# DeltaNet and a two-level mixture of experts: scaled values on VectorE, query masks on GpSimd, scores one chunk further ahead

## The chip, the cores and the metric

The kernel runs on one core of one Trainium2 chip. The metric is device time in microseconds (us) of one execution of the whole program. Four names of engines recur: TensorE (PE in the profile; its weight loads are PEld), VectorE (DVE), ScalarE (ACT) and GpSimd (POOL). SyncE (SP) only issues transfers.

## The reference

Attention first: for each of 4 batches and 8 heads, a 48 by 48 state is carried over 768 steps. Then each of the 3072 rows of 384 numbers goes to one of 16 experts, chosen in two steps (group, then expert in the group). The code is condensed.

```python
k_n = k / (np.linalg.norm(k, axis=-1, keepdims=True) + 1e-06)
for t in range(S):                                     # 768 steps
    y[:, :, t] = q[:, :, t] @ state                    # per batch and head
    v_old = k_n[:, :, t] @ state
    state = state + beta[:, :, t] * outer(k_n[:, :, t], v[:, :, t] - v_old)
x = y.transpose(0, 2, 1, 3).reshape(3072, 384)
g_idx = argmax(x @ w_group)                            # softmax weight g_w
e_idx = argmax(x @ w_expert[g_idx])                    # softmax weight e_w
out[i] = g_w * e_w * (relu(x[i] @ w1[g, e]) @ w2[g, e])
```

## The kernel before

The 768 steps are cut into 24 chunks (`NCH`) of 32 steps (`C`). All 4 batches of a chunk lie on the 128 partitions, 32 each; the 8 heads lie along the free axis, two to a pair. Inside a chunk the recurrence is turned into matrix products, with one triangular 32 by 32 inverse per batch and head. The inverses of four chunks (`RG`) are made together by a generator, `inverse(g)`, as a long row of small VectorE operations; GpSimd makes the square roots of the key norms for it (the result is `nrm`, turned over into `normt`).

One chunk `u` has these steps, in the names of the profile:

- `g_ps` (L278, `gram`): scores of the keys and queries of chunk `u + LEAD` against its keys, made some chunks ahead. They use one buffer, `kqd`, filled by two transfers of 256 KB. ScalarE copies them out as `gt` (keys, for the inverse) and `gq` (queries), both at L288.
- `gqm` (L298, L303, `mask`): the query scores with the upper triangle cut away. For early chunks each is spread to twice the width, with zeros in the half that belongs to the other batch of a pair, so that one product serves two batches.
- `a_ps` (L460, `begin_a`): the values times the negated key norm, eight ScalarE instructions, one for a head, each 128 by 48, written into PSUM. Then (L472) TensorE adds the products of keys and old state to them. ScalarE copies the sum out as `f` (L478).
- `o_ps` (L483): queries times old state.
- `w_ps` (L491): the inverse `mt` times `f`; copied out as `w` (L494).
- `s_ps` (L501): the state products, keys times `w`; copied out as `s_bd` (L507, two instructions). The next chunk's `a_ps` and `o_ps` products read `s_bd`.
- `o_ps` again (L514, or L519 for late chunks): masked query scores times `w`; copied out as `x` (L523), which is the attention output.
- `t_ps`, `xt`, `l_ps`, `lg` (L541 to L554, `logits`): the routing logits of chunk `u - 1`. Every four chunks a ranking product (`hots` and `acc`, into the bank of `l_ps`) is added, and `route(r)` picks the experts by small operations on VectorE and GpSimd. `s_ps` at L703 are small products that sort rows by expert.

The order on each engine's queue is written out by hand: the loop `for u in range(NCH + 1)` (L870) calls the pieces in order, and each engine runs its own instructions strictly in that order. `work(n)` puts as many steps of the running `inverse` and `route` generators into the queues as a budget allows; `allow(...)` releases a generator that holds at a named point. The chunk loop has two forms: one for chunks whose scores are still being made ahead (`if ahead_of[u]`), and an `else` form, in which the logits of the chunk before stand ahead of `w_ps` and of the state products.

PSUM has eight banks. The state `s_ps` takes four; before, `g_ps`, `o_ps`, `t_ps`/`l_ps` have one each, and one (tag `s`) is shared by `a_ps` and `w_ps`.

After the loop the rows are sorted by expert and 16 experts are run one after another (`h_ps`, L1076, and `y_ps`, L1095), fed by transfers of 3 MB of weights for each.

## Time and profile before

| | |
|---|---|
| device time, median of 3 runs | 556.77 us (556.64 to 562.29) |
| the profiled execution: own time, span | 556.0 us, 554.2 us |
| busy: PE, PEld, DVE, ACT, POOL | 477.0, 448.5, 228.1, 211.0, 188.3 us |
| mean granted TensorE clock | 0.926 |
| chunk 1's first state read to the first expert product | 46.9 to 282.9 us |

How to read it: busy time of PE counts modelled ends of pipelined matmuls. A number in brackets after an instruction is the idle time of its engine ahead of it and what ended that. "issue" is time in which an engine waited for nothing that the profile shows. PEclk is the clock that TensorE was granted as a part of the full one. An instruction shown as 32 by 96 "x32" is 32 matmul records; the program lists them as 16, since each fp32 product takes two passes.

### The profile page before, as it was taken

What the parts mean: (1) busy time and instruction counts of PE and PEld (TensorE: products, weight loads), DVE (VectorE), ACT (ScalarE), POOL (GpSimd) and SP (SyncE); (2) the same over time, 40 slices, a digit from 0 to 9 for tenths busy, and PEclk for the clock granted to TensorE, in tenths of its full rate; (3) what the DMA queues carried; (4) which work ended last, traced back from release to release, by engine and by line L of the source; (5) the groups of instructions that cost most, each with busy time, mean ns of one, the idle gap of its engine ahead of it and who ended that gap; (6) DMA issues with size and microseconds to landing.
All of it is one profiled execution on the core that took longest, in us unless ns stands there. A gap on an engine that the chain in (4) does not pass through costs nothing.

```text
span 554.2 us, 19014 instructions
## 1 busy us (share of the span) xinstructions
PE 477.0 (86%) x8124; PEld 448.5 (81%) x8124; DVE 228.1 (41%) x850; ACT 211.0 (38%) x541; POOL 188.3 (34%) x326
## 2 busy tenths in 40 slices
PE   3456888887788776877999999999999999999993
PEld 3346777777777775766799999999999999999993
DVE  3999669189387495412381011101121110111110
ACT  3336675586667566665421111111111111111110
POOL 3040021161341440400114464445653545545322
PEclk9998887799788787787799999999999999999998
DMA  5666665666547343410129878776986788988741
GB/s 168 225 210 165 167 203 149 160 200 171 198 135 227 100 135 95 141 53 17 56 68 311 275 248 286 229 236 217 318 275 209 257 262 282 312 296 258 235 170 34
DMA packets 59593, 107.35 MB, mean 194 GB/s; under 512 B 19438, under 2 KB 41897, under 8 KB 59507
## 3 DMA queue, kind: packets, MB, share of 16 engines
q1 hardware_dynamic: 53587, 96.11, 55.1%
q0 software_dynamic: 5920, 10.00, 5.8%
q8 instruction: 65, 1.06, 0.8%
q14 instruction: 21, 0.17, 0.1%
HBM read 91.97 MB, written 14.27 MB: 192 GB/s over the span
## 4 chain that ended last, share of the span: by engine, by line
PE 50%; DMA 18%; ACT 15%; issue 9%; SPq 4%; DVE 1%; POOL 1%; DVEq 0%; POOLq 0%; ACTq 0%
PE y_ps L1095 11%; PE h_ps L1076 11%; ACT a_ps L460 8%; DMA y_dram<-yq 5%; DMA out_dram<-yo,to_i 5%; PE a_ps L472 5%; PE g_ps L278 4%; PE o_ps L483 4%; DMA yr<-y_dram 4%; PE w_ps L491 4%; SPq L1135 4%; PE l_ps L446 3%; ACT s_bd L507 3%; DMA kqt<-in_kq_dram 2%; PE s_ps L256 2%
## 5 line engine op out<-in xcount | busy, mean ns | idle before, releaser
L1095 PE MATMUL y_ps<-hid,w 128*128 128x224 f32 (+15 forms) x768 | 132.9, 332 | 0.7 <-issue 0.3
L1095 PEld LDWEIGHTS y_ps<-hid,w 128*128 128x128 f32 x768 | 128.9, 190 | 1.8 <-ACT yt L1100 0.8
L1076 PE MATMUL h_ps<-xt,w 128*128 128x232 f32 (+14 forms) x720 | 122.7, 330 | 0.0
L1076 PEld LDWEIGHTS h_ps<-xt,w 128*128 128x128 f32 x720 | 120.1, 190 | 0.3
L1048 POOL DMA_INDIRECT xq<-x_dram,from_q x92 | 87.6, 952 | 34.2 <-issue 25.0
L1079 ACT ACTIVATE hid<-h_ps 128x448 f32<-128x448 f32 (+15 forms) x64 | 32.1, 501 | 99.3 <-PE h_ps L1076 81.2
L1107 POOL DMA_INDIRECT out_dram<-yo,to_i x32 | 34.1, 1064 | 94.4 <-DVE yo L1145 82.4
L1098 DVE COPY yt<-y_ps 128x232 f32<-128x232 f32 (+13 forms) x14 | 5.1, 366 | 140.2 <-PE y_ps L1095 127.7
L460 ACT ACTIVATE a_ps<-kv,normt 128x48 f32<-128x48 f32 x184 | 56.0, 304 | 6.0
L1100 ACT ACTIVATE yt<-y_ps 128x224 f32<-128x224 f32 (+15 forms) x34 | 11.4, 336 | 118.9 <-PE y_ps L1095 91.2
L472 PE MATMUL a_ps<-s_bd,kqt 128*32 128x96 f32 x736 | 29.9, 318 | 12.9 <-ACT s_bd L507 11.2
L507 ACT ACTIVATE s_bd<-s_ps 48x768 f32<-48x768 f32 x46 | 36.8, 799 | 6.1 <-PE s_ps L501 5.8
L472 PEld LDWEIGHTS a_ps<-s_bd,kqt 128*32 128x32 f32 x736 | 25.3, 148 | 14.7 <-ACT s_bd L507 12.5
L501 PE MATMUL s_ps<-w,kv 32*112 32x96 f32 x736 | 27.0, 285 | 7.6 <-ACT found L846 2.7
L501 PEld LDWEIGHTS s_ps<-w,kv 32*112 32x112 f32 x736 | 22.7, 188 | 11.0 <-ACT w L494 3.3
L256 PE MATMUL s_ps<-kqt 48*32 48x32 f32 (+1 forms) x832 | 14.3, 269 | 20.1 <-issue 7.2
L256 PEld LDWEIGHTS s_ps<-kqt 48*32 48x32 f32 x832 | 11.2, 145 | 22.9 <-issue 8.1
L1145 DVE TENSOR_SCALAR yo<-yr,gate 128x384 f32<-128x384 f32 (+14 forms) x28 | 11.1, 420 | 44.9 <-DMA yr<-y_dram 37.8
L446 PE MATMUL l_ps<-wr,xt 128*128 128x20 f32 x132 | 19.2, 273 | 11.0 <-ACT xt L547 9.8
L483 PE MATMUL o_ps<-s_bd,kqt 128*32 128x96 f32 x736 | 27.8, 306 | 0.0
L446 PEld LDWEIGHTS l_ps<-wr,xt 128*128 128x128 f32 x132 | 16.9, 195 | 13.0 <-ACT xt L547 11.2
L278 PE MATMUL g_ps<-kqd,kqt 128*32 128x128 f32 x480 | 24.3, 356 | 3.0 <-issue 2.1
(174 smaller groups left out, 655.3 us busy)
## 6 DMA issues: line engine op xcount, KB each, us to landing
w<-in_w_dram SPq DMA_DIRECT2D x29, 1536.0 KB
kv<-in_kv_dram SPq DMA_DIRECT2D x24, 448.0 KB
kqt<-in_kq_dram SPq DMA_DIRECT2D x20, 512.0 KB
kqd<-in_kq_dram SPq DMA_DIRECT2D x30, 256.0 KB
x_dram<-x SPq DMA_DIRECT2D x24, 192.0 KB
w<-in_w_dram SPq DMA_DIRECT2D x24, 128.0 KB
y_dram<-yq SPq DMA_DIRECT2D x36, 84.0 KB
yr<-y_dram SPq DMA_DIRECT2D x14, 192.0 KB
```

What stands on the lines that cost most here:

```text
L256: nc.tensor.matmul(g_out[quads[b], hh, j, of], lhsT=kqt[rows, 0, j, quads[b]], rhs=kqt[rows, of, j, quads[b]], start=True, stop=True, skip ...
L278: nc.tensor.matmul(g_ps[quads[b], j], lhsT=kqt[:, 0, j, quads[b]], rhs=kqd_[u % 2][:, :, :, j, quads[b]], start=True, stop=True, skip_grou ...
L446: nc.tensor.matmul(out_, lhsT=lhsT, rhs=rhs, start=first, stop=final, skip_group_check=True)
L460: nc.scalar.activation(a_ps[:, h], v[:, h], ACT.Copy, scale=norm[g][:, uu * H + h:uu * H + h + 1])
L472: nc.tensor.matmul(a_ps[quads[b], 2 * j:2 * j + 2, :], lhsT=kqt[:, 0, j, quads[b]], rhs=s_bd[:, b, j], start=False, stop=True, skip_group_ ...
L483: nc.tensor.matmul(o_ps[quads[b], 2 * j:2 * j + 2, :], lhsT=kqt[:, 1, j, quads[b]], rhs=s_bd[:, b, j], start=(j == 0), stop=False, skip_gr ...
L501: nc.tensor.matmul(s_at[0:KR, b, j], lhsT=k[quads[b], j, 0:KR], rhs=w[quads[b], 2 * j:2 * j + 2], start=(u == 0 and j == 0), stop=True, sk ...
L507: nc.scalar.activation(s_bd[rows, :, :, hh, :], s_at[rows, :, :, hh * D:(hh + 1) * D], ACT.Copy)
L1048: nc.gpsimd.indirect_dma_start(out=xq[:, g, :], out_offset=None, in_=x_dram[:, :].rearrange("n (q c) -> (n q) c", q=4), in_offset=bass.Ind ...
L1076: nc.tensor.matmul(h_ps[:, k], lhsT=w1[:, j, (f + k) * 128:(f + k + 1) * 128], rhs=xt[:, j, 0:R], start=(j == 0), stop=(j == DC - 1), skip ...
L1095: nc.tensor.matmul(y_ps, lhsT=w2[:, f, j * 128:(j + 1) * 128], rhs=hid[:, f], start=(f == 0), stop=(f == FC - 1))
L1107: put = nc.gpsimd.indirect_dma_start(out=out[:, :], out_offset=bass.IndirectOffsetOnAxis(ap=to[0:P, i:i + 1], axis=0), in_=yo[0:P, :], in_ ...
```

## The change

Three pieces of work change engine or place, and one constant moves.

- **Scaled values.** `begin_a(u + 1)` is one VectorE multiplication (128 by 384, the norm spread by a stride of zero) where it was eight ScalarE instructions. It writes into a PSUM bank of its own (tag `a`) and stands at the head of chunk `u`, as soon as `f` of chunk `u` has left that bank. Chunk 0 keeps the eight instructions. Before the loop, three products against the identity write that bank (`a_home`), where before they wrote bank 0 of the state.
- **Query masks.** `mask(u)` is a GpSimd multiplication in place on `gq` (128 by 256), queued at the head of the chunk after the one that made the scores. `spread(u + 1)`, at the head of chunk `u`, is two ScalarE copies (128 by 256 each) with a scale of 0 or 1 for each partition; late chunks need none.
- **Scores.** `LEAD` is 10 where it was 9, with one more `kqt` buffer. `gram(u + LEAD)` stands between the state products and the query products; its bank is the one of `w_ps` (tag `s`), the bank `g` is gone, and its copies stand right behind those of the state.
- **The rest.** The first form of the loop now holds for `u < NCH - 3`, so chunks 14 to 20 move from the `else` form into it. The generators start at other chunks, and GpSimd clears the upper triangles of `m` behind the roots where it did so ahead of them.

```diff
-LEAD = 9
+LEAD = 10
@@ gram, keep_scores
-            g_ps = ps.tile([128, NP, 2, 2, C], F32, tag="g", name=f"g_ps{u}")
+            g_ps = ps.tile([128, NP, 2, 2, C], F32, tag="s", name=f"g_ps{u}")
...
                 g_ps = made.pop(u)
+                unmasked.append(u)
@@ mask
         def mask(u):
-            like = [128, H, 2, C]
-            gqm = wk.tile(like, F32, tag="gqm", name=f"gqm{u}", bufs=3)
+            nc.gpsimd.tensor_tensor(raws[u], raws[u],
+                                    cut["causal"][:, None, :].to_broadcast([128, H, C]),
+                                    op=ALU.mult)
+
+        def spread(u):
             if u >= LATE:
...
-                nc.vector.tensor_tensor(gqs[u], raws.pop(u),
-                                        cut["causal"][:, None, :].to_broadcast([128, H, C]),
-                                        op=ALU.mult)
+                gqs[u] = raws.pop(u)
                 return
-            gqs[u] = gqm
-            nc.vector.tensor_tensor(
-                gqs[u], raws.pop(u)[:, :, None, :].to_broadcast(like),
-                cut["upper"].rearrange("p (a t) -> p a t", a=2)[:, None].to_broadcast(like),
-                op=ALU.mult)
+            gqs[u] = wk.tile([128, H, 2, C], F32, tag="gqm", name=f"gqm{u}")
+            for a in range(2):
+                nc.scalar.activation(gqs[u][:, :, a], raws[u], ACT.Copy,
+                                     scale=cut["parity"][:, a:a + 1])
+            raws.pop(u)
@@ begin_a
+            v = kv_[u % NV][:, H * 64:].rearrange("p (h d) -> p h d", h=H)
+            by = norm[g][:, uu * H:(uu + 1) * H]
             if u:
-                a_ps = ps.tile([128, H, D], F32, tag="s", name=f"a_ps{u}")
+                a_ps = ps.tile([128, H, D], F32, tag="a", name=f"a_ps{u}")
+                nc.vector.tensor_tensor(a_ps, v, by[:, :, None].to_broadcast([128, H, D]),
+                                        op=ALU.mult)
             else:
                 a_ps = wk.tile([128, H, D], F32, tag="f", name="f0")
-            for h in range(H):
-                nc.scalar.activation(a_ps[:, h], v[:, h], ACT.Copy,
-                                     scale=norm[g][:, uu * H + h:uu * H + h + 1])
+                for h in range(H):
+                    nc.scalar.activation(a_ps[:, h], v[:, h], ACT.Copy, scale=by[:, h:h + 1])
@@ before the loop
+            for u in range(2 * RG):
+                mask(u)
...
             for u in range(2 * RG, LEAD):
                 early_gram(u, homes[u % len(homes)])
                 begin(after_gram[u])
+                mask(u)
+            spread(0)
@@ the loop over chunks
-                if 0 < u < NCH - 1:
-                    mask(u + 1)
                 if u:
                     next(step)
...
-                keep_scores()
-                if u % RG == RG - 1 and u // RG + 2 < NGR:
-                    start(inverse(u // RG + 2), SHARE)
+                if u + 1 < NCH:
+                    begin_a(u + 1)
+                    spread(u + 1)
+                for v in unmasked:
+                    mask(v)
+                unmasked.clear()
...
-                if ahead_of[u]:
+                if u < NCH - 3:
                     work(10)
                     next(step)
-                    begin_a(u + 1)
                     next(turned)
...
                     next(step)
+                    for v in ahead_of[u]:
+                        gram(v)
+                    keep_scores()
+                    if u % RG == 1 and u // RG + 2 < NGR:
+                        start(inverse(u // RG + 2), SHARE)
                     work(9)
+                    allow(ROOTS)
                     next(step)
                     next(turned)
                     allow(PE_STEP)
                     allow(ACT_STEP)
-                    for v in ahead_of[u]:
-                        gram(v)
                 else:
...
                     next(step)
-                    if u + 1 < NCH:
-                        begin_a(u + 1)
```

ScalarE's queue in chunk 2 before, from the copy `f` of chunk 2 (line, operation, output<-inputs, shape):

```order
L478 ACTIVATE f_1221<-a_ps_1080 128x384
L288 ACTIVATE gt_749<-g_ps_1147 128x2x4x32
L288 ACTIVATE gq_1241<-g_ps_1147 128x2x4x32
L494 ACTIVATE w_1286<-w_ps_1253 128x384
L460 ACTIVATE a_ps_1288<-kv_117,normt_594 128x48 x8
L547 ACTIVATE xt_1301<-t_ps_1297 128x384
L507 ACTIVATE s_bd<-s_ps 48x16x48 x2
L523 ACTIVATE x_1345<-o_ps_1223 128x384
L554 ACTIVATE lg_1089<-l_ps_1347 128x20
```

The same chunk on ScalarE now:

```order
L488 ACTIVATE f_1245<-a_ps_1067 128x384
L305 ACTIVATE gqm_1266<-gq_571,con 128x8x32 x2
L504 ACTIVATE w_1336<-w_ps_1303 128x384
L557 ACTIVATE xt_1342<-t_ps_1338 128x384
L517 ACTIVATE s_bd<-s_ps 48x16x48 x2
L289 ACTIVATE gt_1379<-g_ps_1362 128x2x4x32
L289 ACTIVATE gq_1381<-g_ps_1362 128x2x4x32
L533 ACTIVATE x_1409<-o_ps_1247 128x384
L564 ACTIVATE lg_1118<-l_ps_1411 128x20
```

The eight instructions of the next chunk's `a_ps`, which stood between `w` and the copies of the state, are gone; the two spreads `gqm` stand ahead of `w`, and the copies of the scores have moved from ahead of `w` to behind the state.

TensorE's queue for the same chunk before, from its products with the old state:

```order
L472 MATMUL a_ps_1080<-s_bd,kqt_106 32x96 x16
L483 MATMUL o_ps_1223<-s_bd,kqt_106 32x96 x16
L491 MATMUL w_ps_1253<-f_1221,mt_815 32x48 x32
L541 MATMUL t_ps_1297<-con,x_1140 128x128 x3
L501 MATMUL s_ps<-w_1286,kv_119 112x96 x16
L514 MATMUL o_ps_1223<-w_1286,gqm_995 64x48 x16
L446 MATMUL l_ps_1347<-wr,xt_1301 128x20 x3
L278 MATMUL g_ps_1352<-kqd_116,kqt_104 32x128 x16
```

And now:

```order
L482 MATMUL a_ps_1067<-s_bd,kqt_106 32x96 x16
L493 MATMUL o_ps_1247<-s_bd,kqt_106 32x96 x16
L501 MATMUL w_ps_1303<-f_1245,mt_867 32x48 x32
L551 MATMUL t_ps_1338<-con,x_1194 128x128 x3
L511 MATMUL s_ps<-w_1336,kv_120 112x96 x16
L278 MATMUL g_ps_1362<-kqd_116,kqt_104 32x128 x16
L524 MATMUL o_ps_1247<-w_1336,gqm_1069 64x48 x16
L454 MATMUL l_ps_1411<-wr,xt_1342 128x20 x3
```

The score products `g_ps` moved from the end of the chunk to right behind the state products; nothing else on TensorE moved here.

GpSimd's queue ahead of the loop before, from the clearing of `acc` to the first root operation (`r`) of the second inverse:

```order
L799 MEMSET acc 128x16
L800 COPY what<-con 128x24x2
L801 COPY sel<-con 128x512
L324 MEMSET m_761 128x16x16
L324 MEMSET m_761 128x2x8x8
L324 MEMSET m_761 128x4x4x4
L324 MEMSET m_761 128x8x2x2
L324 MEMSET m_761 128x16
L335 ISA
L335 TENSOR_TENSOR r_776<-r_775 128x32
```

And now, from the last four of the first eight masks on:

```order
L294 TENSOR_TENSOR gq_310<-gq_310,con 128x256
L294 TENSOR_TENSOR gq_349<-gq_349,con 128x256
L294 TENSOR_TENSOR gq_384<-gq_384,con 128x256
L294 TENSOR_TENSOR gq_427<-gq_427,con 128x256
L811 MEMSET acc 128x16
L812 COPY what<-con 128x24x2
L813 COPY sel<-con 128x512
L294 TENSOR_TENSOR gq_760<-gq_760,con 128x256
L294 TENSOR_TENSOR gq_800<-gq_800,con 128x256
L341 TENSOR_TENSOR r_827<-r_826 128x32
```

Ten masks stand ahead of the roots of the second inverse, and the five clears of `m` have gone behind them.

More of the change, by code (lines that the diff above doesn't have):

```diff
@@ L36, in constants @@
     out = {
-        "upper": np.concatenate([np.where(np.arange(2)[None, :, None] == b % 2, (i < k)[:, None], 0)
-                                 .reshape(C, 2 * C) for b in range(n_batch)], axis=0),
         "causal": np.tile(i < k, (n_batch, 1)),
@@ L41, in constants @@
         "eps": np.full((128, 1), 1e-6),
+        "parity": np.stack([p // C % 2 == b2 for b2 in range(2)], axis=1),
         "ident": (p[:, None] == p[None, :]),
@@ L333, in inverse @@
                                         float(0x5f3759df), op0=ALU.mult, op1=ALU.add)
+                yield NEXT if g > 1 else 0
                 for _ in range(3):
@@ L807, in deltanet_then_moe @@
                 begin(after_gram[u])
-            for n in (H * D, H * D, H * D // 2):
-                nc.tensor.matmul(s_ps[:, 0, 0:n], lhsT=ident, rhs=con[:, cols[1]:cols[1] + n],
+                mask(u)
+            spread(0)
+            a_home = ps.tile([128, H * D], F32, tag="a", name="a_home")
+            for n in (H * D // 2, H * D, H * D):
+                nc.tensor.matmul(a_home[:, 0:n], lhsT=ident, rhs=con[:, cols[1]:cols[1] + n],
                                  start=True, stop=True, skip_group_check=True)
             second = inverse(1)
-            start(second, 0.95)
+            start(second, 0.78)
             while 0 not in mts:
@@ L815, in deltanet_then_moe @@
                 allow(ACT_STEP)
-            mask(0)
             allow(ROOTS)
```

26 lines of the change are left out of this document (13 added, 13 removed).

## The prediction

> **What bounds the kernel now.** I read busy time by stage first, cutting the span where the chain of waits shows chunk 1, 14 and 21 begin to read the old state and where the first expert begins. The columns are: stretch, length, then busy time (and instructions) of PE, PEld, DVE, ACT, POOL, the granted clock, the share of the DMA engines, GB/s.
>
> ```profile
> 46.90:173.40 126.50, 106.35 (x3057) 94.63 (x3052) 91.71 (x381) 86.85 (x225) 30.83 (x97) 0.86 0.60 179
> 173.40:242.70 69.30, 52.76 (x1660) 47.23 (x1651) 38.00 (x150) 43.72 (x113) 18.62 (x51) 0.82 0.39 116
> 242.70:282.90 40.20, 33.53 (x863) 29.46 (x864) 13.96 (x72) 19.06 (x50) 2.15 (x2) 0.79 0.10 31
> 282.90:554.20 271.30, 261.97 (x1562) 259.85 (x1561) 47.37 (x96) 43.86 (x99) 125.83 (x141) 0.99 0.76 244
> ```
>
> The experts, the last row, keep TensorE at 262 of 271 us, and no line of theirs changes: 271.3 us stay. The change lives in the three rows above it: 13 chunks in 126.5 us (9.7 each), 7 in 69.3 (9.9 each), and the last three with the sort in 40.2. There PE is idle for 20.2, 16.5 and 6.7 us, and its clock is 0.79 to 0.86 of the full one.
>
> Next I asked what PE waits for in the chunks (total us, times, longest):
>
> ```profile
> PE a_ps L472 <- ACT s_bd L507: 11.2, 7, 2.4
> PE l_ps L446 <- ACT xt L547: 9.8, 11, 1.0
> PE l_ps L446 <- ACT lg L554: 8.9, 5, 2.6
> ```
>
> All three are ScalarE copies. The timeline of one chunk at full clock shows what holds them up (start, length, engine):
>
> ```profile
> 115.85 0.90 PE L472 MATMUL a_ps<-s_bd,kqt 128*32 128x96 f32 x31
> ...
> 117.48 0.88 PE L491 MATMUL w_ps<-f,mt 32*32 32x48 f32 x64
> ...
> 118.43 0.49 ACT L494 ACTIVATE w<-w_ps 128x384 f32<-128x384 f32 x1 [0.27 <-PE w_ps L491]
> ...
> 118.95 2.66 ACT L460 ACTIVATE a_ps<-kv,normt 128x48 f32<-128x48 f32 x8
> ...
> 119.77 1.04 PE L501 MATMUL s_ps<-w,kv 32*112 32x96 f32 x32 [0.74 <-ACT a_ps L460]
> ...
> 120.74 1.14 PE L514 MATMUL o_ps<-w,gqm 64*64 64x48 f32 x32
> ...
> 121.92 1.61 ACT L507 ACTIVATE s_bd<-s_ps 48x768 f32<-48x768 f32 x2
> ...
> 122.07 0.84 PE L446 MATMUL l_ps<-wr,xt 128*128 128x20 f32 x6 [0.20 <-ACT xt L547]
> ...
> 122.85 1.08 PE L278 MATMUL g_ps<-kqd,kqt 128*32 128x128 f32 x32
> ...
> 123.74 0.68 PE L472 MATMUL a_ps<-s_bd,kqt 128*32 128x96 f32 x24
> ```
>
> The state products end at 120.81, but ScalarE is inside its eight `a_ps` instructions (2.66 us) and starts `s_bd` only at 121.92, after `xt`. `l_ps` waits for `xt`, and the next chunk for `s_bd`. The period is 123.74 - 115.85 = 7.89 us.
>
> That is not 9.7, so I looked at the clock and at the stalls in the chain of waits, and at busy time in windows of 3.41 us, the grid on which the clock steps:
>
> ```profile
> 69.74 1.00 issue
> ...
> 104.75 1.87 PE g_ps L278 x32
> ...
> 115.03 1.01 PE g_ps L278 x32
> ...
> 134.37 0.66 PE a_ps L472 x32
> ...
> 151.17 0.94 issue
> ...
> 173.43 1.28 PE a_ps L472 x32
> ...
> 222.94 0.79 issue
> ```
>
> ```profile
> 99.92:103.33 3.41, 1.47 (x28) 1.24 (x24) 0.00 (x0) 3.27 (x8) 0.00 (x0) 1.00 0.66 239
> 103.33:106.75 3.42, 3.11 (x48) 2.87 (x52) 0.68 (x4) 0.64 (x4) 1.36 (x5) 0.50 0.04 14
> ...
> 120.40:123.81 3.41, 3.21 (x93) 2.97 (x89) 3.41 (x23) 3.28 (x8) 0.02 (x1) 1.00 0.87 318
> ```
>
> A window in which PE was busy for 1.47 us is followed by one at half clock; one with 3.21 us is not. At half clock the same 32 products take 1.87 us for 1.01 and 1.28 for 0.66. A clock of 0.86 over 126.5 us means 126.5 x 0.14 x 2 / 3.41 = 10.4 windows at half clock; 0.82 over 69.3 us means 7.3. I price a window at 1.2 us: a chunk of 6.9 us of PE steps grows to about 10.5 when its large groups near double and its waits and small products do not, so 3.41 us do the work of 2.2. Bounds: 0 (something else was late anyway) and 1.6 (everything near doubles).
>
> From the first quoted stall "issue" to the second there are five of 0.94 to 1.60 us (with one of 0.37 ahead of them, 6.5 us); the third is the only one of the next stage. These terms rebuild the first stage: 13 x 7.89 = 102.6, three rankings at 8.9 / 5 = 1.8 are 5.4, issue 6.5, ten windows 12.5; sum 127.0, measured 126.5. So I trust them for the forecast.
>
> **The change part by part.** *Full-clock period, chunks 1 to 13.* From `a_ps` to `w_ps` stays 117.48 - 115.85 = 1.63. From `w_ps` to the end of `w` is 1.44, and I let the state products follow after 0.05: ScalarE has nothing behind `w` that they could wait for (the 0.85 seen here goes with `a_ps` in the row's own bracket). The rest of PE's row is the same four groups in another order: 0.97 (state, start to start) + 1.14 + 0.78 + 0.89 = 3.78. Sum 6.90. ScalarE's side is shorter: state products 1.04, `s_bd` 1.61, together 2.65 against 3.78, so the score products behind the state now hide `s_bd`. The removed wait leaves VectorE as next: 91.71 / 13 = 7.05 us of work in a chunk. I take 7.05.
>
> *What VectorE gains and loses.* Rows by shape:
>
> ```profile
> L303 DVE TENSOR_TENSOR gqm<-gq,con 128x512 f32<-128x512 f32 x14 | 9.4, 675 | 0.0
> L298 DVE TENSOR_TENSOR gqm<-gq,con 128x256 f32<-128x256 f32 x9 | 3.7, 411 | 0.0
> L288 ACT ACTIVATE gq<-g_ps 128x256 f32<-128x256 f32 x15 | 6.4, 428 | 0.0
> L680 POOL TENSOR_TENSOR mine<-hots,what 128x384 f32<-128x384 f32 x4 | 3.8, 944 | 0.3
> ```
>
> The masks leave (13.1 us in these rows), 23 multiplications of 128 by 384 come. Between 411 and 675 ns I take 550: 12.7 us. That they write PSUM is in no row; a tenth more or less is 1.3 us in all. So VectorE's 7.05 stands. But `begin_a` now stands in VectorE's strict queue, among the rows of the inverses, and TensorE's next `a_ps` waits for it; ahead of it VectorE can be late by some five us, the rest of the chunk, before TensorE notices.
>
> *Spread on ScalarE*: two of 128 by 256, by the `gq` row 428 ns each, 0.86, between `f` and `w`. Its cover is `w_ps` (0.88). With 490 ns each (the `w` row, a wider copy) it would be 0.1 late, 1.3 us over 13 chunks; I take nothing. ScalarE loses 2.66 and gains 0.86 a chunk.
>
> *Masks on GpSimd*: 944 / 384 x 256 is about 630 ns; 23 of them, 14.5 us, on an engine busy 30.8 of 126.5 us, needed some nine chunks later: nothing on the path in the loop.
>
> ```profile
> 40.52 0.20 DVE L392 TENSOR_TENSOR t_c<-m 128x28 f32<-128x28 f32 x1
> ...
> 119.33 0.31 DVE L392 TENSOR_TENSOR t_c<-m 128x28 f32<-128x28 f32 x1
> ...
> 117.16 3.27 POOL L621 TENSOR_SCALAR at<-con,low 128x128 f32<-128x128 f32 x4
> ```
>
> The same small VectorE instruction takes 0.31 while GpSimd is in a long one, 0.20 while it is idle: at worst a half more. I count none of it. The Trainium skill (GPSIMD Engine Reference, section "8. Key points") speaks against this move: GpSimd shares its SBUF interfaces with VectorE and contends with VectorE instructions that have two SBUF inputs. The pair above agrees in sign; by that rule at its worst VectorE would stop for all 14.5 us, and the sum would be that much later.
>
> *Before the loop.* Ten masks (6.3 us by 0.63) stand ahead of the second roots on GpSimd, whose queue ends this work at 36.4 now:
>
> ```profile
> 36.22 0.22 POOL L340 TENSOR_SCALAR nrm<-r 128x32 f32<-128x32 f32 x1
> 36.86 6.05 DMA kqd<-in_kq_dram
> ```
>
> So `nrm` comes near 43.5, and behind it the first `begin_a` near 45.5. Beside it the first score products wait for `kqd` until 42.9, with one more load of 512 KB queued ahead of those four of 256 KB: 3.0 us at their pace (1 MB in 6.05), of which I take 1.9, as they shared that time with what was queued before. So to 44.8, then come the score and query products: `a_ps` of chunk 1 near 47.4 for 46.9. Cost 0.5, bounds 0 and 4.
>
> *Chunks 14 to 20* have no scores now or before, and change to the first form. PE from state to next chunk is short, so ScalarE ends last: 1.63 + 1.49 + 1.04 + 1.61 + 0.05 = 5.82. The `else` form had this wait, with `lg` queued behind `a_ps`:
>
> ```profile
> 219.98 0.69 PE L446 MATMUL l_ps<-hots,con 128*128 128x64 f32 x2 [2.64 <-ACT lg L554]
> ```
>
> *Chunks 21 and 22* keep the `else` form but lose the 2.66 each: 5.3.
>
> **The sum.** Chunks 1 to 13: 13 x 7.05 = 91.7, rankings 5.4, issue 6.5 as now, and windows at half clock. Of PE's idle time the two waits that go (11.2 + 9.8 us) are about half, so I take 6 windows for 10.4: 7.2. Sum 110.8, a gain of 15.7. Chunks 14 to 20: 7 x 5.82 = 40.7, two rankings 3.6, issue 0.8, 4 windows 4.8; sum 49.9, a gain of 19.4. Last chunks 5.3. Start -0.5. In all 39.9 us, from 556.0 us (the profiled execution: span 554.2 and 1.8 around it; the median is 0.8 higher): **516 us**. Its own range, with 2 to 10 windows in the first stage and 1 to 7 in the second and the start's bounds, is 507 to 528.
>
> **The rivals.** *The clock never falls.* If what remains of PE's idle time never fills enough of a window, the ten windows left (12 us) go: 504; with those of the last stage (0.79 over 40.2: five, 6 us) 498. For it: every window at full clock with 3 us or more of PE was followed by full clock. Against: rankings and issue stalls remain. The Trainium skill (TensorE: Matmul & The Clock Gate, section "HAM oscillation — how this bites in real kernels") has the clock fall only after a PE gap of over about 3.4 us. By that rule this rival holds, for no such gap would be left; the trace disagrees, since the window with 1.47 us busy sufficed. Chance 0.15.
>
> *VectorE's waits come onto the path.* These are its waits in the chunks now:
>
> ```profile
> DVE place L661 <- POOL rk L629: 28.4, 4, 9.2
> DVE m L319 <- ACT gt L288: 13.4, 4, 4.6
> DVE r L365 <- POOL nrm L340: 8.8, 4, 4.6
> ```
>
> They cost nothing as long as nobody waits for VectorE. With 7.05 us of work in a 7.05 us chunk it has no room to make them up, and `begin_a` is queued behind them. If the two that belong to the inverse (22.2 us) land on the path: 538. Against: they end when VectorE is ahead, and a late VectorE does not wait. Chance 0.2.
>
> *Slower.* The same mechanism in full: all 50.6 us of those waits stand ahead of a `begin_a`, GpSimd's queue being longer by its masks, and the sum gains 16 us of contention: 516 + 50.6 + 14.5 = 581. It decides for slower once more than 46 us of VectorE's waits reach TensorE, over 2 us in each of 20 chunks. Half of these are long waits for the routing, which have a chunk of slack. Chance 0.05.
>
> *Half clock throughout.* Then PE bounds: 13 x 10.5 + 11.9 = 148.4 (22 more than now), less 5 in each later stage: 568. Nothing in the windows shows denser PE work lowering the clock. Chance 0.04.
>
> *No change.* The "issue" stalls (7.3 us up to chunk 20) grow six times, as PE asks for its instructions sooner beside transfers whose share goes from 0.60 to 0.69: 553. Chance 0.04.
>
> **How the numbers follow.** The forecast keeps 0.52. The likeliest is 516. With the second rival inside and half of the first, 0.8 is held by 500 to 541. Faster by over 1% (below 551, about what a measurement of this kernel can tell): 0.52 + 0.15 + 0.2 = 0.87; within 1%: 0.04; slower: 0.05 + 0.04 = 0.09.
>
> **What would show it.** Right: chunks of 7 to 8.5 us with scores and 6 to 7 without; the waits of PE for `s_bd` and `xt` near zero; the granted clock of the first stage above 0.9; the first expert product near 243 us. Wrong: PE's `a_ps` waiting for VectorE by more than a few us in all (second rival), `w_ps` waiting for `mt`, a first `a_ps` later than 50 us, a clock at or below 0.86 with the waits gone, or issue stalls well above 8 us. If the experts' stage is not 271 us, the sum misses something that I have not seen.

## The result, and the profile after

The changed kernel takes 534.48 us (median of 4 runs, 526.48 to 538.19), the kernel before 557.30 beside it: a ratio of medians of 0.959. Counting only the fast runs (526.48 and 531.08 us of the changed kernel), the ratio is 0.950, 95% interval 0.941 to 0.958, and so are all the ratios below. The forecast was 516 us with a range of 500 to 541. The profiled execution is the quickest of the four: 526.48 us, with a span of 524.7.

Here is busy time by stage, cut at the same marks as before: chunks 1 to 13, chunks 14 to 20, the last chunks with the sort, the experts. Columns: stretch, length, busy time of PE, PEld, DVE, ACT, POOL, granted clock, share of the DMA engines, GB/s.

```profile
49.55:168.19 118.64, 98.55 (x3053) 85.29 (x3050) 100.44 (x413) 68.17 (x145) 45.41 (x111) 0.94 0.61 185
168.19:219.55 51.36, 45.21 (x1655) 39.71 (x1654) 36.17 (x139) 26.08 (x54) 21.74 (x52) 0.93 0.45 140
219.55:252.74 33.19, 28.46 (x863) 24.54 (x864) 15.71 (x76) 14.49 (x35) 2.16 (x2) 0.95 0.14 47
252.74:524.70 271.96, 262.29 (x1563) 260.00 (x1561) 47.77 (x97) 43.93 (x99) 125.91 (x141) 0.99 0.75 243
```

Chunks 14 to 20 gave 18 us and the last chunks 7, both near the forecast. Chunks 1 to 13 gave 8, half of what was forecast. The start lost some 3 us. What PE waits for between the first state product and the first expert has changed its kind (total us, times, longest):

```profile
PE g_ps L278 <- issue: 6.2, 3, 2.5
PE w_ps L501 <- issue: 5.4, 6, 1.6
PE s_ps L511 <- issue: 5.2, 4, 3.2
PE o_ps L529 <- issue: 3.3, 5, 1.4
PE o_ps L524 <- issue: 2.9, 2, 1.7
PE a_ps L482 <- ACT s_bd L517: 2.6, 4, 1.2
PE l_ps L454 <- ACT lg L564: 2.1, 5, 0.8
PE s_ps L511 <- ACT xt L557: 1.0, 1, 1.0
```

The three copies of ScalarE held PE for 29.9 us before and for 5.7 now. In their place stands "issue": an engine that waits for nothing the profile shows. A piece of the chain of waits of the changed kernel (start, length) has the longest of these stalls, in the middle of the state products:

```profile
94.52 0.88 PE w_ps L501 x64
95.42 0.50 ACT w L504
95.97 0.83 PE s_ps L511 x21
96.80 3.25 issue
100.05 0.88 PE s_ps L511 x11
100.92 1.87 PE g_ps L278 x32
```

All 32 products need the same `w`, so it cannot be that 21 of them were ready and the other 11 not. The `g_ps` behind the stall also runs at half clock (1.87 us for 1.01).

The DMA records show what ends it. One queue, named "instruction" in the profile, moves single packets of 16,384 bytes: 44 of them between the first state product and the first expert product, in both kernels. This is a reading of all stalls in chunks 1 to 13 of the changed kernel that are over 0.3 us (12, 17.7 us in all), put beside the packet that began last ahead of each one's end (us; not a view of the profile):

```
stall ends  long  packet begins  from there to the end
 55.99      1.86    53.64          2.35
 67.01      1.74    64.64          2.37
 71.81      0.96    69.32          2.49
 80.58      1.56    77.94          2.64
100.05      3.25    97.78          2.27
112.11      1.82   109.86          2.25
122.22      2.48   119.85          2.37
132.63      1.19   130.33          2.30
138.44      0.82   136.09          2.35
155.60      0.77   153.01          2.59
160.64      0.37   158.32          2.32
164.78      0.85   162.38          2.40
```

Every stall ends 2.25 to 2.64 us behind the start of such a packet, whatever its length. So I took these packets for TensorE's own instructions. The Trainium skill (Runtime: NRT & Kernel Launch, section "Instruction fetch mechanics") says that an engine's instructions are brought in blocks of 16 KiB, 256 instructions, while the current ones run, at a cost that is mostly hidden. The size agrees with the packets; that the cost is hidden does not hold here.

### The profile page after: what moved, and what is told of

It is laid out like the page before. It is cut to its first block, busy times and chain, and to the rows that moved or that the text cites. A ratio compares the mean times of both kernels' runs of the same rounds, so it can differ in the third digit from the quotient of the medians.

```text
span 524.7 us, 19069 instructions
## 1 busy us (share of the span) xinstructions
PE 459.7 (88%) x8188; PEld 428.8 (82%) x8188; DVE 235.0 (45%) x849; ACT 170.5 (32%) x386; POOL 215.7 (41%) x350
## 4 chain that ended last, share of the span: by engine, by line
PE 68%; DMA 11%; issue 10%; ACT 5%; POOL 3%; SPq 1%; another core or an unknown queue 1%; DVE 1%; DVEq 0%; POOLq 0%; ACTq 0%
PE y_ps L1109 18%; PE h_ps L1090 18%; DMA out_dram<-yo,to_i 6%; PE s_ps L511 4%; PE w_ps L501 4%; PE a_ps L482 4%; PE o_ps L493 4%; PE g_ps L278 3%; PE o_ps L524 3%; PE l_ps L454 3%; ACT s_bd L517 2%; PE s_ps L256 2%; DMA yr<-y_dram 2%; DMA kqt<-in_kq_dram 2%; PE t_ps L551 2%
## 5 line engine op out<-in xcount | busy, mean ns | idle before, releaser
L1121 POOL DMA_INDIRECT out_dram<-yo,to_i x32 | 34.1, 1065 | 94.1 <-DVE yo L1159 79.6
L294 POOL TENSOR_TENSOR gq<-gq,con 128x256 f32<-128x256 f32 x24 | 26.2, 1098 | 61.3 <-ACT gq L289 43.6
L256 PE MATMUL s_ps<-kqt 48*32 48x32 f32 (+1 forms) x896 | 15.8, 272 | 21.1 <-issue 7.2
L511 PE MATMUL s_ps<-w,kv 32*112 32x96 f32 x736 | 25.7, 268 | 7.5 <-issue 5.2
L511 PEld LDWEIGHTS s_ps<-w,kv 32*112 32x112 f32 x736 | 21.5, 172 | 11.2 <-issue 6.4
L501 PEld LDWEIGHTS w_ps<-f,mt 32*32 32x32 f32 x1536 | 20.6, 113 | 11.5 <-issue 7.6
L501 PE MATMUL w_ps<-f,mt 32*32 32x48 f32 x1536 | 24.9, 214 | 5.4 <-issue 5.4
L400 DVE TENSOR_TENSOR t_d<-m 128x16 f32<-128x16 f32 (+14 forms) x90 | 27.8, 312 | 0.2
L406 DVE TENSOR_TENSOR m<-m,t_b 128x16 f32<-128x16 f32 (+14 forms) x90 | 27.3, 303 | 0.2
L400 DVE TENSOR_TENSOR t_b<-m 128x16 f32<-128x16 f32 (+14 forms) x90 | 27.1, 301 | 0.0
L406 DVE TENSOR_TENSOR m<-m,t_d 128x16 f32<-128x16 f32 (+14 forms) x90 | 26.5, 294 | 0.2
L278 PE MATMUL g_ps<-kqd,kqt 128*32 128x128 f32 x448 | 18.5, 303 | 8.8 <-issue 6.2
```

What stands on the lines that cost most here:

```text
L256: nc.tensor.matmul(g_out[quads[b], hh, j, of], lhsT=kqt[rows, 0, j, quads[b]], rhs=kqt[rows, of, j, quads[b]], start=True, stop=True, skip ...
L278: nc.tensor.matmul(g_ps[quads[b], j], lhsT=kqt[:, 0, j, quads[b]], rhs=kqd_[u % 2][:, :, :, j, quads[b]], start=True, stop=True, skip_grou ...
L400: nc.vector.tensor_tensor(tv, left.to_broadcast([128] + like), right.to_broadcast([128] + like), op=ALU.mult)
L406: nc.vector.tensor_tensor(to, to, tv, op=ALU.add)
L501: nc.tensor.matmul(w_ps[q, h], lhsT=mt[q, uu * H + h], rhs=f[q, h], start=(h == 0), stop=True, skip_group_check=True)
L511: nc.tensor.matmul(s_at[0:KR, b, j], lhsT=k[quads[b], j, 0:KR], rhs=w[quads[b], 2 * j:2 * j + 2], start=(u == 0 and j == 0), stop=True, sk ...
```

## The experiments

The first theory was the prediction's: the gain is what VectorE's scaled values take off ScalarE, and the clock's windows. The second, from the profile after: TensorE now waits for its instructions, whose blocks come late beside the loads of keys and queries. Each of the runs below stood beside runs of the kernel before on the same chip, and its ratio is to those.

### What each part of the change is worth

**The changed kernel again**, to have a second profile and a measure on the chip of the next three.

> The changed kernel as it is, for a second profile and more times. The theory (TensorE, no longer held up by ScalarE, now waits for its own instructions, which come in blocks of 16 KB): 524 to 540 us, with 'issue' stalls of TensorE between the first state read and the first expert product of 18 to 30 us where the kernel before has 7.5; each stall ends 2.2 to 2.8 us after a block's transfer begins; the times that are longer have more stalls or more half-clock windows. The rival (VectorE or GpSimd came onto the path): the stalls change little, and TensorE's waits that end in a VectorE or GpSimd instruction are over 5 us.

530.68 us (528.32 to 534.34), ratio 0.958 (0.952 to 0.964). Its chunks 1 to 13 took 124.4 us, 5.8 more than in the first profile, with the same stalls (16.5 us) but ten windows at half clock for four.

**Scaled values back on ScalarE**, at the old place in the queue.

```diff
-                nc.vector.tensor_tensor(a_ps, v, by[:, :, None].to_broadcast([128, H, D]),
-                                        op=ALU.mult)
+                for h in range(H):
+                    nc.scalar.activation(a_ps[:, h], v[:, h], ACT.Copy, scale=by[:, h:h + 1])
@@ the loop: begin_a(u + 1) again behind w (first form), behind the logits (else form)
```

> The scaled values go back to eight ScalarE instructions behind w, all else as changed (own bank, masks, scores, loop forms). The theory: ScalarE's 2.66 us come back between w and the state copies, in a chunk with scores about 1 us beyond what the query and score products hide, in one without about 2.5: 545 to 555 us, and the 'issue' stalls fall to 8 to 14 us, because blocks of instructions arrive while TensorE waits for ScalarE. The rival (the gain came from the place of the scores and the form of the loop): within 1% of the changed kernel.

546.32 us, ratio 0.986 (0.979 to 0.992): 15.6 us slower than the changed kernel beside it. Its first three stages, in the columns of the first table:

```profile
49.91:168.53 118.62, 100.84 (x3052) 86.29 (x3050) 89.49 (x379) 93.75 (x247) 50.56 (x110) 0.92 0.62 186
168.53:229.59 61.06, 47.62 (x1654) 41.93 (x1654) 33.60 (x132) 41.81 (x112) 20.78 (x52) 0.89 0.40 122
229.59:269.43 39.84, 32.81 (x863) 28.75 (x863) 14.55 (x74) 19.03 (x51) 2.15 (x2) 0.79 0.10 31
```

Chunks 14 to 20 and the last ones give back 16 us; chunks 1 to 13 take the same 118.6. PE's waits in these:

```profile
PE a_ps L482 <- ACT s_bd L517: 3.3, 6, 0.6
PE l_ps L454 <- ACT lg L564: 3.3, 2, 1.8
PE g_ps L278 <- issue: 3.1, 2, 1.8
PE o_ps L493 <- ACT x L533: 2.7, 7, 0.4
```

Waits for ScalarE are back, and the stalls over 0.3 us are 7.1 us for 17.7 (7.8 up to the first expert, just under the expected 8 to 14). The removed wait had been traded for another one.

**Scores back at the end of the chunk**, with their copies and the start of the inverse.

```diff
@@ the loop, first form
-                    for v in ahead_of[u]:
-                        gram(v)
-                    keep_scores()
-                    if u % RG == 1 and u // RG + 2 < NGR:
-                        start(inverse(u // RG + 2), SHARE)
                     work(9)
                     allow(ROOTS)
                     next(step)
                     next(turned)
                     allow(PE_STEP)
                     allow(ACT_STEP)
+                    for v in ahead_of[u]:
+                        gram(v)
+                    keep_scores()
+                    if u % RG == 1 and u // RG + 2 < NGR:
+                        start(inverse(u // RG + 2), SHARE)
```

> The score products, and with them their copies, go back to the end of the chunk; all else as changed. The theory: the copies then stand ahead of f on ScalarE and cost some 0.5 us in each of 13 chunks, of which the stalls for instructions give part back: 527 to 542 us, waits of TensorE for f or the score copies of 4 to 8 us. The rival (hiding the state copies behind the scores is the main thing): 12 chunks or more lose over 1 us each, 545 us or more.

530.78 us, ratio 0.957 (0.951 to 0.964), for 530.68 of the changed kernel: the place of the scores makes no difference that these runs can tell. The time lies in the expected range, but the reason given for it does not: of the 4 to 8 us of waits for `f` or the score copies none appears in chunks 1 to 13.

**Masks on VectorE**, in place and at the same points of the code.

```diff
-            nc.gpsimd.tensor_tensor(raws[u], raws[u],
+            nc.vector.tensor_tensor(raws[u], raws[u],
```

> The masks are made by VectorE at the same places of the code (128 by 256, in place); the spread stays on ScalarE. The theory (VectorE is not on the path in the loop, GpSimd is ahead of it): the loop stays within 2 us, the first a_ps of chunk 1 comes 2 to 4 us earlier (46 to 48), as GpSimd's ten masks no longer stand ahead of the second roots; 520 to 536 us. The rival (VectorE is as busy as TensorE, so 10 us more of it show): 8 to 12 us slower than the changed kernel, with waits of TensorE for VectorE.

535.53 us, ratio 0.963 (0.958 to 0.969). A miss at the start: the first state product came at 54.0 us (in the longest of the four runs, which is the profiled one), not earlier. VectorE's strict queue is the reason: the last of the ten masks waits 3.3 us for ScalarE's `gq` and starts at 37.5 us, and the second inverse's first instruction on VectorE (`m`, L320) stands behind it at 38.0, where it came at 29.5 us in the changed kernel. By the ratios the masks on GpSimd are worth some 3 us (0.963 against 0.958), and the intervals overlap.

**The old loop form for chunks 14 to 20.**

```diff
-                if u < NCH - 3:
+                if ahead_of[u]:
```

> Only the loop's form for chunks 14 to 20 is put back: the branch without grams, with the scaled values begun behind its logits. Theory (that form's order had left ScalarE's row of copies on the path, and the scaled values on VectorE already took the worst of it away): chunks 14 to 20 take 53 to 58 us in place of 51.4, all other stages as in the changed kernel, 531 to 538. Rival (the whole gain of chunks 14 to 20, 18 us, is the form's): 69 us there, 545 to 550. Second rival (the form is nothing): 51 us, 528 to 532.

526.42 us, ratio 0.956 (0.950 to 0.962), where the changed kernel had 0.950 and 0.958; 51.5 us in chunks 14 to 20. The first theory's 53 to 58 fell, and the second rival (51) holds for the stage: the gain of those chunks is not the form's. The device time lies below every range that was given.

### Are the instructions what TensorE waits for

**More instructions for the same products.** The state products are split by head.

```diff
@@ a_ps; o_ps likewise
-                        nc.tensor.matmul(a_ps[quads[b], 2 * j:2 * j + 2, :],
-                                         lhsT=kqt[:, 0, j, quads[b]], rhs=s_bd[:, b, j],
-                                         start=False, stop=True, skip_group_check=True)
+                        for hh in range(2):
+                            nc.tensor.matmul(a_ps[quads[b], 2 * j + hh, :],
+                                             lhsT=kqt[:, 0, j, quads[b]], rhs=s_bd[:, b, j, hh],
+                                             start=False, stop=True, skip_group_check=True)
```

> The state products are split, 16 of 96 columns into 32 of 48 for each of the two sums, the same arithmetic: 128 more TensorE instructions in a chunk, 466 to 594. Theory (supply of instructions): blocks in the loop rise from 44 to some 55, and with 1.2 us of stall for each of the added ones and no slack left, issue stalls rise from 22 to 35 us or more; together with at most 0.4 us of added TensorE work in each of 22 chunks the time is 545 to 565. Rival (the stalls come from what the other engines do): stalls stay at 18 to 26 us, and the time is at most 9 us over that of the changed kernel (530 to 540).

578.79 us, ratio 1.049 (1.043 to 1.056): 48 us more in the profiled execution (574.13), and slower than the kernel before. PE's two largest waits in chunks 1 to 13:

```profile
PE w_ps L504 <- issue: 17.3, 7, 5.1
PE s_ps L514 <- issue: 10.6, 3, 3.6
```

55 blocks came in for 44. Up to the first expert the stalls over 0.3 us grew from 23.5 to 48.5 us, and the windows at half clock from 7 to 22: 15 of them at the prediction's 1.2 us are 18 us. That is 43 of the 48 and leaves 5 for the products themselves. 2816 added records in 22 chunks and 11 added blocks make 64 bytes an instruction. The theory's time (545 to 565) was too low because it left the clock out.

**The same instructions without the loads.** The loop's loads of keys and queries are left out; those of `kv` stay. The output is another, and the experts get other counts, so of its one execution (773.62 us) only what stands ahead of the experts is compared.

```diff
@@ load_kq, block: kq_d[u] -> kq_d[u % 2]; load_kv: kv_d[u] -> kv_d[u % 2]
@@ the end of a chunk
-                if ahead_of.get(u + 2):
-                    block(u + 2 + LEAD)
-                if 0 < u < NCH - NB:
-                    load_kq(u + NB)
```

> The loop's loads of keys and queries are left out: every chunk reads the keys, queries and values of chunk 0 or 1 again, so the output is another, and the experts' stage may get other counts; only chunks 1 to 20 are read. Theory (TensorE now waits for its own instructions, which arrive as blocks of 16 KB, 44 in the loop): the blocks are as many as before, so if a block is late by itself, TensorE's issue stalls stay near 22 us (18 to 26) and chunks 1 to 13 near 118 to 124 us. First rival (the blocks are late because they share the DMA engines with the loads of keys, queries and values): the stalls fall to 10 us or less and chunks 1 to 13 to 106 to 112 us. Second rival (the stalls are nothing to do with blocks): they no longer end some 2.2 to 2.8 us behind a block's start.

Here is the row of chunks 1 to 13 in busy time by stage, and then every wait of PE in them:

```profile
50.27:150.46 100.19, 92.80 (x3052) 81.33 (x3050) 95.19 (x385) 67.37 (x145) 46.72 (x106) 0.98 0.29 95
```

```profile
PE a_ps L482 <- DVE a_ps L466: 2.7, 2, 2.3
PE w_ps L501 <- DVE t_b L400: 2.1, 1, 2.1
PE w_ps L501 <- issue: 0.9, 3, 0.4
PE l_ps L454 <- ACT lg L564: 0.6, 2, 0.3
PE s_ps L511 <- issue: 0.2, 1, 0.2
```

As many blocks (24 in this stage) cost 1.1 us of stalls for 18, the clock is 0.98, and the stage takes 100.2 us for 118.6, less than the 106 to 112 expected. So in this stage the blocks are late beside these loads. They are not the whole of it: chunks 14 to 20 have no such loads in either kernel, and the stalls over 0.3 us there are still 2.8 us in this run, for 4.2; in the last chunks they are 2.4, for 1.6. With the stalls gone VectorE is what PE meets next, as the prediction had it, though only in three waits of 4.8 us in all.

**The kernel before, without the same loads.**

> The kernel before with its loop's loads of keys and queries left out (every chunk reads the data of chunk 0, so the output is another; only chunks 1 to 20 are read). Theory (the kernel before was bound by ScalarE's wait and by few late blocks): chunks 1 to 13 fall from 126.8 to 108 to 118 us (13 of 7.89, rankings 5.4, up to 8 windows at half clock), with TensorE's waits for s_bd and xt as before; so the change is worth 8 to 18 us there once instructions come in time (100.2 in the changed kernel without these loads). Rival (the moved work has no part in it, supply alone sets both): 98 to 104 us.

The same two views of this kernel (one execution, 850.83 us, read like the one above):

```profile
44.83:162.85 118.02, 101.29 (x3061) 91.15 (x3057) 89.42 (x368) 86.33 (x224) 30.95 (x97) 0.88 0.25 83
```

```profile
PE l_ps L446 <- ACT xt L547: 11.2, 12, 1.0
PE l_ps L446 <- ACT lg L554: 2.5, 2, 1.3
PE w_ps L491 <- issue: 1.8, 1, 1.8
```

The top of the expected 108 to 118 us: ScalarE's waits stay, and so do eight windows at half clock. Between the two kernels without these loads lie 118.0 - 100.2 = 17.8 us, of which some 8 are seven fewer windows at half clock. That is what the change is worth in chunks 1 to 13 when the instructions come in time; with the loads it was 8.

### Further versions

**The loads of a chunk in three bursts.** A chunk's 1.66 MB stood in one row of SP's queue.

```diff
@@ behind gram(v), in the first form
+                    if ahead_of.get(u + 2):
+                        block(u + 2 + LEAD)
@@ behind w, in the first form, for the chunk before
+                    if 1 < u <= NCH - NB:
+                        begin([of_kq(u - 1 + NB)])
@@ the end of a chunk
-                if ahead_of.get(u + 2):
-                    block(u + 2 + LEAD)
-                if 0 < u < NCH - NB:
-                    load_kq(u + NB)
```

> The same loads, but a chunk's 1.66 MB no longer stand in SP's queue as one burst at the chunk's end: kqd is queued right behind the scores that free it, kv and the store of x at the chunk's end as now, and kqt in the next chunk behind a one-column write by ScalarE after w. Theory (a block of TensorE's instructions waits behind what the burst has queued on the DMA engines): bursts of 0.5 to 0.66 MB hold a block up for at most 2 us in place of 5, issue stalls before the first expert fall from 20 to 24 us to 12 or less, chunks 1 to 13 take 106 to 114 us for 118.6 to 125.4, and the time is 515 to 524. Rival (only the amount that is moved counts, not how it is spread): stalls stay at 18 to 26 us, 526 to 532. Slower: kqd or kqt come late for the scores, TensorE's g_ps waits for a DMA, over 535.

518.01 us (517.12 to 518.99), ratio 0.941 (0.935 to 0.946). The time is in the expected range; the stalls are not (15.6 us before the first expert, for 12 or less), nor are chunks 1 to 13 (116.9 us, for 106 to 114). PE's stalls in chunks 1 to 13:

```profile
PE g_ps L278 <- issue: 3.8, 2, 2.0
PE w_ps L501 <- issue: 3.6, 2, 2.0
PE s_ps L511 <- issue: 2.3, 2, 1.4
PE o_ps L524 <- issue: 1.1, 2, 0.8
```

That is 10.8 us in these rows (10.4 by stalls over 0.3 us, for 17.7). How the loads are spread counts, then, but so does their amount.

**Masks behind the second roots** on GpSimd, all but the first two, and one load behind four others.

```diff
-            for u in range(2 * RG):
+            for u in range(2):
                 mask(u)
...
             for u in range(2):
                 block(u + LEAD)
+            begin([of_kq(2 * RG + 3)])
+            for u in range(2, LEAD):
+                mask(u)
```

> Masks 2 to 9 are queued on GpSimd behind the second roots, not ahead of them, and the load of kqt 11 behind kqd's blocks. Theory (the ten masks of 1.1 to 1.28 us ahead of the loop put nrm, and with it the first state product, 2 to 3 us late): first state product at 46.5 to 47.5 in place of 49.5, the rest as before, gain of 2 to 3 us (526 to 529). Rival (the start hangs on ScalarE's and VectorE's own rows, or the masks run into the first chunks): start stays at 49 to 50, or the gain is lost by waits of the first scores for gq; 529 to 533.

523.99 us, ratio 0.950 (0.945 to 0.956), for 526.42 of the old loop form on the same chip; the intervals overlap, and the time is below the expected 526 to 529. The first state product came at 47.8 us for 49.6 (expected 46.5 to 47.5): 1.7 us of the 2 to 3.

**Both.**

> Both edits at once: the masks behind the second roots and the loads in three bursts. Theory (they act in different places, so they add): 2 us less than the three bursts alone, first state product at 47.5 to 48.5, 512 to 522. Rival (the earlier start only meets a later load): the same time as the three bursts alone.

515.26 us (511.28 to 520.94), ratio 0.934 (0.925 to 0.942), for 518.01 of the bursts alone. The gain of 2.7 us is what was expected, but the spread of these runs is larger than it. The first state product came at 45.3 us, ahead of the expected 47.5 to 48.5 (profile of the longest run, 520.94 us).

**Fewer instructions on top of both.** Chunks 14 to 23 use the spread masks too.

```diff
-            if u >= LATE:
-                gqs[u] = raws.pop(u)
-                return
@@ advance
-                if u + LEAD < NCH:
+                if True:
                     for b in pairs:
```

> On top of masks behind the roots and loads in three bursts: chunks 14 to 23 use the spread masks too (two more copies on ScalarE a chunk), so their query products are 16 of 64 rows for 32 of 32 rows by head and batch: 32 matmuls and 32 weight loads fewer in a chunk, about 4 KB of TensorE's instructions, 2 to 3 blocks fewer before the first expert. Theory (supply): stalls in chunks 14 to 20 fall from 4.2 to 6.7 us to 2 to 4, the time is 510 to 514. Rival (ScalarE's two added copies of 0.49 us come onto the path, as ScalarE ends last in those chunks): chunks 14 to 20 take 51 to 56 us, the time is 516 to 522.

517.15 us (515.35 to 518.95), with the kernel before at 557.90 beside it: ratio 0.927 (0.923 to 0.932), the lowest of all. Since the kernel before differs by 8 us between the two sets, the ratios are what to compare, and the intervals of the last two overlap: a gain from this edit is not shown. The time expected (510 to 514) was missed; it is the rival's (516 to 522), but the stage is the theory's. Chunks 14 to 20 took 47.4 us at full clock, with 2.5 us of stalls over 0.3 us:

```profile
160.82:208.21 47.39, 43.33 (x1431) 38.63 (x1430) 36.76 (x139) 31.60 (x68) 22.01 (x55) 1.00 0.49 152
```

ScalarE's two added copies a chunk (31.60 us busy for 26.08) stay hidden.

## Why the prediction was right, and where it was wrong

The time fell by 4 to 5% and lies in the range; the sum was 10.4 us short of the profiled execution. That the median lies in the range is in part luck: it is some 18 us above the 516, and above the sum's own range of 507 to 528. The range reaches 541 because of VectorE's waits, which did not come. By the prediction's own signs, chunks 1 to 13 took 9.1 us each and not 7 to 8.5, the first expert came at 252.7 us and not near 243, and the issue stalls, 23.5 us up to it, were well above 8. These are its terms beside what they measured (us; windows as the clock's steps count them; stalls over 0.3 us; the rest is the stage less its stalls and 1.2 us a window):

```
                               forecast           measured           difference
first a_ps of chunk 1          47.4               49.55               +2.15
chunks 1-13: rest              97.1               96.1                -1.0
             issue stalls       6.5               17.7               +11.2
             half clock         7.2 (6 windows)    4.8 (4 windows)    -2.4
chunks 14-20: rest             44.3               44.8                +0.5
             issue stalls       0.8                4.2                +3.4
             half clock         4.8 (4)            2.4 (2)            -2.4
last chunks and sort           34.9               33.2                -1.7
experts                       271.3              272.0                +0.7
```

**The step that failed** is "issue 6.5 as now", and "issue 0.8" in the next stage: together 14.6 us too low, of which the other terms gave 4.2 back. The stalls of before were taken as a fixed cost. I read them as a race: a block is asked for ahead of its use, and the kernel before, waiting for ScalarE in each chunk, mostly had it by then. Once the wait goes, PE reaches the block's first instruction sooner and waits for it. No record shows when a block was asked for, but the stalls in chunks 1 to 13 move as the race would have them: with ScalarE's wait back they are 7.1 us, without the loads 0.4, with 128 more instructions a chunk 34.1. The rival called "no change" named this mechanism; it was given 0.04 and six times the stalls, where it came to three times.

**The period's size was right, its reason only in part.** The rest, worked out for chunks 1 to 13 of the runs in the same way:

```
                              stage    stalls  windows   rest
before                        126.8      6.8     10.1    107.8
before, no loads              118.0      1.8      8.0    106.6
scaled values on ScalarE      118.6      7.1      5.2    105.3
after                         118.6     17.7      4.0     96.1
after, again                  124.4     16.5     10.0     95.9
scores late                   119.4     12.2      9.4     95.9
old loop form                 125.4     16.6     11.0     95.6
masks behind the roots        124.8     12.6     12.0     97.8
three bursts                  116.9     10.4      8.0     96.9
fewer instructions            115.8     14.1      5.0     95.7
after, no loads               100.2      0.4      1.2     98.4
```

Stages from 100 to 127 us fall into two groups: 105 to 108 with the scaled values on ScalarE, 96 to 98 with them on VectorE, against 97.1 forecast (13 x 7.05 and the rankings). Three profiles that are not in the table fall in with the second group: 98.0 with both edits, 95.1 with the masks on VectorE, 99.1 with more instructions. So VectorE's multiplication is worth 9 us there (105.3 to 96.1), and all other parts of the change together at most 3 (107.8 to 105.3); the scores' place shows nothing. It also bears out 1.2 us for a window, a price that was set before any of these runs. The reason given, VectorE's 7.05 us of work in a chunk, is not borne out as the bound. VectorE was busy for 100.4 us in this stage, 7.7 a chunk and more than the whole rest of 96.1, and it went on through PE's stalls. PE's own row of 6.90 fits the rest as well (13 x 6.90 and the rankings are 95.1). From chunk 1 on, only the run without loads has PE wait for VectorE by more than 0.2 us at a time. One more reading does not hold: of the 11.2 us of waits for `s_bd` in the kernel before, 10.9 lie in chunks 14 to 20 and none in chunks 1 to 13, where PE waited for `xt` (8.8 us).

**The clock.** The forecast took six windows in chunks 1 to 13 for ten. The profiles of the changed kernel and its near relatives have 4 to 12, so the term was no more than a middle value. It is what sets the two profiles of the same kernel apart in this stage: they differ by 5.8 us, and six windows at 1.2 us less 1.2 us of stalls are 6.0. The first rival (the clock never falls) was false: windows with stalls of 1.2 to 3.3 us were enough to lower it.

**Chunks 14 to 20** came out as forecast, but not for the reason of the new order alone: with the old form 51.5 us, with ScalarE's scaled values 61.1. The rest is 47.5 us with the old form and 44.8 with the new one, so the form's share is about 3 us, and stalls that shift hide it in the total.

**The start** cost more than the 0.5 us taken, inside the bounds of 0 to 4. GpSimd's queue in the changed kernel:

```profile
32.55 6.38 POOL L294 TENSOR_TENSOR gq<-gq,con 128x256 f32<-128x256 f32 x5 [3.91 <-ACT gq L261]
...
45.28 0.22 POOL L346 TENSOR_SCALAR nrm<-r 128x32 f32<-128x32 f32 x1
```

`nrm` came at 45.5 us where 43.5 was forecast (its own terms, 36.4 and 6.3, make 42.7), as a mask was priced at 0.63 us. Over the whole span its fastest, median and slowest are these (ns):

```profile
L294 POOL TENSOR_TENSOR gq<-gq,con x24: 722/774/5788, 23.0 to 168.1; 128x256 f32<-128x256 f32 x24
```

It is 0.77 in the middle, and 1.28 each in the five at the start, where VectorE works all the time:

```profile
32.50:38.90 6.40, 4.71 (x132) 3.49 (x133) 6.26 (x14) 4.62 (x18) 6.35 (x6) 1.00 0.45 155
```

But `nrm` alone does not set the start. In the second profile of the changed kernel it came at 43.7 us, as forecast, and the first state product at 50.0. There the five masks take 3.69 us in all and VectorE pays. The first row is the kernel before, the others are this profile:

```profile
30.18 0.30 DVE L392 TENSOR_TENSOR t_d<-m 128x144 f32<-128x144 f32 x1
...
31.86 0.83 DVE L400 TENSOR_TENSOR t_d<-m 128x144 f32<-128x144 f32 x1
...
43.25 1.50 PE L501 MATMUL w_ps<-f,mt 32*32 32x48 f32 x64 [3.11 <-DVE mt L441]
```

The same VectorE instruction takes 0.83 us beside the masks for 0.30, the inverse `mt` is ready at 43.2 us for 38.2, and TensorE's first `w_ps` waits 3.1 us for it. So the term that was missing at the start is the contention of the two engines, of which the prediction counted nothing. Why GpSimd paid in one execution and VectorE in the other is open. The rule on the shared SBUF interfaces that it weighed (the Trainium skill, GPSIMD Engine Reference, section "8. Key points") agrees in kind. In the loop, too, VectorE pays (last section), but nobody waits for it there.

**The other rivals.** VectorE's waits did not come onto the path from chunk 1 on. In chunks 1 to 20 VectorE waits for ScalarE, and so is ahead of it:

```profile
DVE a_ps L466 <- ACT f L488: 18.3, 5, 5.6
DVE m L320 <- ACT gt L289: 9.3, 4, 2.7
```

PE waits for VectorE once, for 0.2 us. The slower case needed 46 us of such waits (its text speaks of 16 us of contention, its sum has 14.5). Half clock throughout did not come either: the mean granted clock was 0.94 in the first stage.

## What to carry to other kernels

When a wait that comes back in every chunk is taken away, price again the waits that it covered: a stall that is small and rare now may be small because the engine was late anyway. Where many small matmuls run beside bulk loads, TensorE's instruction stream is itself a load that has to arrive: here 128 more instructions a chunk cost 48 us, and loads in three short rows and not in one brought the ratio from 0.950 and 0.958 to 0.941. Split a stage into steady work, stalls and clock windows before comparing two runs; the first was the steadiest measure here of what an edit is worth (95.6 to 98.4 us in stages of 100 to 125).

## What was not expected of the hardware

- TensorE's instructions come in blocks of 16 KB, and PE goes on 2.25 to 2.64 us after a late block's transfer begins (12 stalls of chunks 1 to 13), while the transfer itself takes about 1 us (0.9 to 1.6 in 66 packets). What delays the block's start beside the loads is open: the records show when a transfer begins and not when it was asked for. Ahead of the 3.25 us stall the DMA engines were 0.89 busy until the block began, at 97.78 us:

```profile
97.00:97.70 0.70, 0.00 (x0) 0.00 (x0) 0.70 (x4) 0.00 (x0) 0.54 (x3) 1.00 0.89 328
97.70:98.80 1.10, 0.00 (x0) 0.00 (x0) 1.10 (x4) 0.00 (x0) 0.85 (x4) 1.00 0.53 197
```

- A late block can cost twice (12 stalls in chunks 1 to 13, four windows at half clock). The window on the clock's grid that holds most of this stall is followed by one at half clock:

```profile
96.87:100.29 3.42, 0.24 (x9) 0.24 (x9) 3.42 (x12) 0.00 (x0) 2.70 (x12) 1.00 0.53 199
100.29:103.70 3.41, 3.41 (x60) 2.76 (x58) 3.34 (x10) 2.44 (x4) 0.00 (x0) 0.50 0.04 14
103.70:107.11 3.41, 3.13 (x86) 2.91 (x86) 1.04 (x2) 1.31 (x5) 0.69 (x3) 1.00 0.89 204
```

  The seven windows at half clock up to the first expert follow windows with PE busy for 0.24, 1.60, 1.78, 1.97, 2.02, 2.24 and 2.80 us; others with 1.84 and 2.21 us were followed by full clock. So no single amount decides, and none of the seven was idle throughout, as the Trainium skill (TensorE: Matmul & The Clock Gate, section "What's actually happening") has it for a fall of the clock.
- A two-input GpSimd instruction stretches a VectorE instruction that runs beside it. The same VectorE form without and with a mask beside it, in the changed kernel:

```profile
76.43 0.20 DVE L400 TENSOR_TENSOR t_c<-m 128x28 f32<-128x28 f32 x1
...
147.72 0.73 POOL L294 TENSOR_TENSOR gq<-gq,con 128x256 f32<-128x256 f32 x1
147.74 0.75 DVE L400 TENSOR_TENSOR t_c<-m 128x28 f32<-128x28 f32 x1
```

  Up to the first expert 20 VectorE instructions are more than 0.2 us longer than the median of their form, 10.5 us in all, and each stands beside a GpSimd `TENSOR_TENSOR` of over 0.65 us. With the masks on VectorE there are three. GpSimd can pay as well: its slowest mask took 5.79 us.
